# Value products of three key tiles in one visit to the TensorE queue, with a new table for the side work

## The chip, the cores and the metric

The kernel runs on one core of one Trainium2 chip. The metric is the device time of one execution in microseconds; lower is better. Before the change the median of 3 runs is 819.45 us (817.82 to 821.63).

## What is computed

Three blocks follow each other. The first, attention over 4 x 8 heads with the queries averaged in pairs, is where the change lies:

```python
q_pool = q.reshape(B, H, S // factor, factor, D).mean(axis=3)
scores = scale * np.matmul(q_pool, k.transpose(0, 1, 3, 2))
scores = scores - np.max(scores, axis=-1, keepdims=True)
attn = np.exp(scores)
attn = attn / (np.sum(attn, axis=-1, keepdims=True) + 1e-09)
return np.matmul(attn, v).astype(np.float32)
```

Sequence 1152 (576 pooled queries, 1152 keys), head width 64. The second block is a soft mixture of 8 experts over the 2304 resulting rows of 512 (logits `x @ phi`, softmax over the rows for the slots, softmax over the slots for the way back); the third is a gated feed-forward block with three weight matrices that arrive as 64-bit numbers.

## The kernel before

**Pairs and tiles.** Attention is done for 16 pairs of heads, p = 0 to 15. A pair has 9 key tiles of 128 keys (kt, 0 to 8), two heads (s) and two halves of 288 queries (h). For each (kt, s, h), `qk` issues two matmuls on TensorE (`sc`, L376 and L378): the product itself in split precision, with the negated row maximum as an extra row of the second. ScalarE takes the exponential (`e`, L384). GpSimd adds the `e` tiles of a head over the key tiles (`acc`, L413). `av` (L419) multiplies `e` by the values: for one tile and one half, two matmuls with 64 output rows each, one per head. A stretch of `av` matmuls between two stretches of scores is called a visit here.

**The maximum of the next pair.** While pair p is worked on, `max_tile` computes the plain scores of pair p+1 (`mxp`, L335) in 27 pieces, and VectorE reduces each (`mx`, L336). `max_row` turns the result (`mxw` on VectorE L340, `mxt` on TensorE L342, `mrow` on ScalarE L344) and `send_row` sends it with two small DMAs to where the second score matmul of the next pair reads it.

**Order.** Pairs 0 and 15 (`HALVED`) are done one query half at a time; pairs 1 to 14 follow the list `STEP`. In each key tile: four scores (`q0` to `q3`), a maximum piece after each (`m`; how many there are in which tile is in `MAX`), the value products of the tile before (`a0`, `a1`), the two additions (`e0`, `e1`). The products of the last tile follow right behind those of tile 7.

**Side work.** Everything else of the pairs around p is put between these steps by the table `AT`: a time of 4.59 means key tile 4, at the first step whose place in the list is past .59. Every engine works through its instructions in the order in which this program issues them. Among the side work: `low_k`, `low_q` (VectorE: the low parts of the split), `fill_w`, `spread_q`, `send_q`, `block_q`, `load_k/q/v` (DMAs, all from SyncE's queue), `sums` and `recips` (denominators), `x_turn`, `x_divide`, `x_logits`, `x_share`, `logit_add` (output rows and expert logits of pair p-1), the `d_` and `slot_` steps in p = 5, 9 and 13. The 64-bit weights are turned into 32-bit ones here, 36 tiles in all, called doubles below: `load_64` starts the DMA (up to three in a pair), `abs_64` does two ScalarE steps (L690, L692), and two `turn_64` steps on VectorE follow (L694, L695). Pairs 1 to 7, 9, 11 and 13 have three doubles, pairs 8, 10 and 12 two, pair 14 none.

**PSUM.** Scores, maximum pieces and all turned tiles share six banks (`bank`, tag `u`), given out in turn; `av` has two banks of its own. So TensorE can be at most six results ahead of the engines that read them.

Of the kernel before, what the change touches and what calls it, by code (L numbers as in the profile page):

```python
# [19 lines left out]
NKT = 9  # L20
# [7 lines left out]
NG = 6  # L28
NF = 12

STEP = "q0 m q1 m q2 m q3 m a0 a1 e0 e1".split()
MAX = [4, 4, 3, 4, 4, 4, 4, 0, 0]
EDV = []
XDV = []
AT = dict(
    spread_q=2.7,
    low_k=[0.6, 1.6],
    low_q=3.55,
    send_q=4.4,
    fill_w=[2.1, 3.2, 6.1],  # L40
    load_v=7.3,
    max_row=7.4,
    send_row=8.2,
    drop_k=7.0,
    load_q=4.3,
    load_k=5.73,
    sum_q=5.91,
    high_q=6.6,
    block_q=7.05,
    round_k=[7.8, 8.6],  # L50
    take_x=0.55,
    sums=2.6,
    recips=3.58,
    x_turn=[4.6, 5.6, 6.6],
    x_divide=[4.6, 5.6, 6.6],
    x_logits=7.6,
    x_share=8.3,
    logit_add=8.5,
    d_turn=0.59,
    d_exp=1.6,  # L60
    d_back=2.59,
    d_copy=3.55,
    slot_part=4.59,
    slot_copy=5.55,
    slot_turn=6.61,
    c_soft=[2.6, 4.6, 5.6],
    load_64=[0.86, 1.65, 4.0],
    abs_64=[2.6, 3.8, 7.6],
    turn_64=[3.6, 4.6, 5.6, 6.6, 7.1, 7.7, 8.1, 8.6],
    load_ew=[1.0, 3.4],  # L70
    load_14=[0.7, 1.7, 2.2, 2.7, 3.7, 4.2, 4.7, 5.7, 6.2, 7.7],
    load_15=[0.5, 1, 1.5, 2, 2.5, 3, 3.5, 4, 4.5, 5.5, 5.84, 6, 6.5, 7, 7.5, 8, 8.5],
)
AT_0 = dict(
    round_k1=[1.06, 1.56],
# [63 lines left out]
def attention_softmoe_gated_kernel(ctx: ExitStack, tc: tile.TileContext, kT, qT, vv, ip, cst, w1, w2, wg, wv, wo, rg, out):  # L139
# [640 lines left out]
    with tc.manual_schedule():  # L780
# [78 lines left out]
        for p in range(NP):  # L859
# [6 lines left out]
            for u, (kt, h) in enumerate(steps):  # L866
# [3 lines left out]
                for i, step in enumerate(order):  # L870
# [8 lines left out]
                    elif step == "m":  # L879
                        if mx < quota:  # L880
                            next_max(p, mx)
                            mx += 1
                    elif step[0] == "e":
                        add_e(p, kt, n, h)
                    elif h is None and kt:
                        av(p, kt - 1, n)
                    elif h is not None and u >= LAG:
                        av(p, *steps[u - LAG])
            for i, (kt, h) in enumerate(steps[-LAG:] if p in HALVED else ((NKT - 1, 0), (NKT - 1, 1))):
                if p == NP - 1 and i == LAG - 1:  # L890
                    sums(p, (1,))
                av(p, kt, h)
# [407 lines left out]
```

## Time and profile before

| | |
|---|---|
| median of 3 runs | 819.45 us |
| the profiled execution, its own time | 811.85 us |
| its span, first to last instruction | 810.1 us |
| busy in the span: TensorE matmul, VectorE, ScalarE, GpSimd | 763.3, 530.5, 474.2, 502.3 us |
| mean granted TensorE clock | 0.978 of full speed |
| pairs 1 to 14 | from 62.0 to 524.5 us |

The profile is of one execution. Its page gives for each engine the busy time and, per group of instructions, the number, the mean length and the idle time of the engine before them with what ended it. A row of the timeline gives the start, the length, the engine, the line, the operation, the tile written and read and, in brackets, the idle time before it. TensorE's matmuls overlap their successors, so the distance from start to start says more there than the length. An `av` matmul is recorded twice, since it is done in 32-bit floating point.

### The profile page before, as it was taken

The numbers are of one execution on the slowest core, as the hardware profiler recorded it, in microseconds if no ns is written. First come the engines' busy times: TensorE is split into PE (matmuls) and PEld (weight loads), VectorE is DVE, ScalarE is ACT, GpSimd is POOL, SyncE is SP. The second block draws the span as 40 slices with busy tenths as digits, with TensorE's granted clock in tenths as the row PEclk, the third lists the DMA queues.
The fourth block names the chain that finished last, engine by engine and source line by source line (L and its number), as shares of the span: only waits on it lengthen the run. The fifth ranks groups of instructions, "written<-read, shape, count | busy, mean of one in ns | idle before, by whom it ended". The sixth has DMA issues, their size and how long they took to land.

```text
span 810.1 us, 14487 instructions
## 1 busy us (share of the span) xinstructions
PE 763.3 (94%) x4861; PEld 536.4 (66%) x4861; DVE 530.5 (65%) x933; ACT 474.2 (59%) x1255; POOL 502.3 (62%) x393
## 2 busy tenths in 40 slices
PE   5889999999999999899998999998999999999998
PEld 4546667666566666566766667664436788888887
DVE  7648779887698887769778778555205575445330
ACT  3337777667667676666766666564316685645330
POOL 5557888786777888667877778742202785444330
PEclk8889999999999999999999999998999999999999
DMA  8668898898999999789898786657999010000001
GB/s 233 144 165 213 219 216 243 240 243 219 215 268 260 238 242 234 213 223 229 222 218 231 206 206 170 191 185 242 321 375 364 1 40 26 27 27 27 26 27 40
DMA packets 100875, 150.44 MB, mean 186 GB/s; under 512 B 28864, under 2 KB 61760, under 8 KB 100800
## 3 DMA queue, kind: packets, MB, share of 16 engines
q1 hardware_dynamic: 100800, 149.50, 66.3%
q8 instruction: 39, 0.64, 0.3%
q14 instruction: 36, 0.29, 0.1%
HBM read 89.39 MB, written 13.11 MB: 127 GB/s over the span
## 4 chain that ended last, share of the span: by engine, by line
PE 65%; DVE 14%; DMA 9%; issue 5%; ACT 3%; SPq 2%; POOL 1%; ACTq 0%; POOLq 0%; DVEq 0%
PE yo L1204 18%; PE av L419 12%; PE sc L376 9%; PE mxp L335 7%; DVE mx L336 6%; PE sc L378 6%; PE gv L1156 3%; DMA m<-mrow 3%; DVE w L694 2%; DVE qs L304 2%; DVE w L695 1%; PE xo L465 1%; DMA vt<-in_vv_dram 1%; PE hin L973 1%; ACT e L384 1%
## 5 line engine op out<-in xcount | busy, mean ns | idle before, releaser
L413 POOL TENSOR_TENSOR acc<-acc,e 128x576 f32<-128x576 f32 (+1 forms) x232 | 329.9, 1441 | 78.1 <-ACT e L384 77.1
L384 ACT ACTIVATE e<-sc 128x288 f32<-128x288 f32 x576 | 223.1, 413 | 163.7 <-PE sc L378 146.5
L336 DVE TENSOR_REDUCE mx<-mxp 128x1 f32<-128x384 f32 x432 | 216.2, 546 | 69.9 <-PE mxp L335 66.9
L376 PE MATMUL sc<-m,ws 128*128 128x288 f32 x576 | 192.6, 339 | 11.5 <-DVE mx L336 8.5
L378 PE MATMUL sc<-m,ws 65*128 65x288 f32 (+1 forms) x576 | 172.0, 303 | 6.7 <-DMA m<-mrow 6.1
L419 PE MATMUL av<-e,vt 128*64 128x288 f32 x1152 | 173.8, 423 | 0.0
L376 PEld LDWEIGHTS sc<-m,ws 128*128 128x128 f32 x576 | 111.5, 194 | 88.0 <-issue 36.3
L335 PE MATMUL mxp<-kh,bd 128*128 128x384 f32 x432 | 155.2, 368 | 12.8 <-DVE bd L809 6.8
L378 PEld LDWEIGHTS sc<-m,ws 65*128 65x128 f32 (+1 forms) x576 | 111.3, 193 | 8.4 <-DMA m<-mrow 4.7
L419 PEld LDWEIGHTS av<-e,vt 128*64 128x64 f32 x1152 | 70.1, 137 | 58.7 <-issue 27.3
L335 PEld LDWEIGHTS mxp<-kh,bd 128*128 128x128 f32 x432 | 85.0, 198 | 22.9 <-DVE mx L336 9.1
L1161 DVE SCALAR_TENSOR_TENSOR th<-th,gv 128x384 f32<-128x384 f32 x72 | 39.8, 553 | 61.9 <-ACT th L1158 61.3
L1204 PE MATMUL yo<-woh,hW 128*128 128x512 f32 (+1 forms) x228 | 73.9, 385 | 0.0
L1204 PE MATMUL yo<-woh,hA 128*128 128x512 f32 (+1 forms) x228 | 71.9, 380 | 0.0
L1187 POOL TENSOR_TENSOR hW<-hu,hW 128x384 fp32r<-128x384 f32 x36 | 36.5, 1016 | 49.8 <-ACT hW L1186 49.5
L413 POOL TENSOR_TENSOR acc<-e,e 128x576 f32<-128x576 f32 x28 | 40.7, 1473 | 39.8 <-ACT e L384 28.4
L1158 ACT ACTIVATE th<-gv 128x384 f32<-128x384 f32 x72 | 35.2, 488 | 42.8 <-PE gv L1156 40.2
L694 DVE SCALAR_TENSOR_TENSOR w<-w,raw 128x512 uint32<-128x512 uint32 x36 | 40.9, 1135 | 26.2 <-ACT raw L692 26.2
L1187 POOL TENSOR_TENSOR hA<-hu,hA 128x384 fp32r<-128x384 f32 x36 | 36.5, 1015 | 30.3 <-ACT hA L1186 25.9
L695 DVE SCALAR_TENSOR_TENSOR w<-raw,w 128x512 uint32<-128x512 uint32 x36 | 50.8, 1412 | 0.3
L474 ACT ACTIVATE xt<-xo,rr 96x64 f32<-96x64 f32 x186 | 42.5, 307 | 13.5 <-PE xo L465 12.4
L1204 PEld LDWEIGHTS yo<-woh,hW 128*128 128x128 f32 x228 | 42.1, 188 | 8.2 <-issue 0.7
(164 smaller groups left out, 943.4 us busy)
## 6 DMA issues: line engine op xcount, KB each, us to landing
w<-in_w_dram SPq DMA_DIRECT2D x88, 256.0 KB
ws<-kh SPq DMA_DIRECT2D x96, 192.0 KB
w<-in_w_dram SPq DMA_DIRECT2D x20, 512.0 KB
ws<-kraw SPq DMA_DIRECT2D x96, 96.0 KB
vt<-in_vv_dram SPq DMA_DIRECT2D x16, 576.0 KB
qraw<-in_qT_dram SPq DMA_DIRECT2D x15, 576.0 KB
m<-qh SPq DMA_DIRECT2D x60, 144.0 KB
kraw<-in_kT_dram SPq DMA_DIRECT2D x15, 576.0 KB
```

Of the source, the lines that this page charges most:

```text
L335: pe.matmul(o, lhsT=bds[p][:, t, :], rhs=kh[p][:, KC * c:KC * c + KC], start=True, stop=True)
L336: dv.reduce_max(out=mx3[p][:, t, c:c + 1], in_=o, axis=AX.X)
L376: pe.matmul(o, lhsT=w[:, s, 0, k], rhs=high_parts(p, s, h), start=True, stop=False)
L378: pe.matmul(o, lhsT=w[0:n, s, 1, k], rhs=low_parts(p, s, h)[0:n], start=False, stop=True)
L384: ac.activation(e, o, AF.Exp, scale=0.0625)
L413: eng.tensor_tensor(out=t, in0=a, in1=e, op=ALU.add)
L419: pe.matmul(avt[p, h][64 * s:64 * s + 64, 0:HQ], lhsT=vt[p][:, kt, 64 * s:64 * s + 64], rhs=ets[p, kt, s, h], start=(kt == 0), stop=(kt == ...
L474: ac.activation(xts[j // 3][:, j % 3, p % 4, c], o[:, i, c], AF.Copy, scale=r[:, j, s:s + 1])
L694: lambda y=y, lo=lo: dv.scalar_tensor_tensor(out=y, in0=y, scalar=3, in1=lo, op0=ALU.logical_shift_left, op1=ALU.bitwise_or),
L695: lambda y=y, hi=hi, key=key: (dv.scalar_tensor_tensor(out=y, in0=hi, scalar=0x80000000, in1=y, op0=ALU.bitwise_and, op1=ALU.bitwise_or), ...
L1187: gp.tensor_tensor(out=b, in0=u, in1=f(a), op=ALU.subtract)
L1204: pe.matmul(o, lhsT=x, rhs=w[:, c], start=(ft == 0 and i == 0), stop=(ft == NF - 1 and i == 2))
```

## The change

The two steps `a0 a1` of `STEP` become one step `a`, which does nothing except in tiles 2, 5 and 8: there it issues the value products of this tile and the two before it, both halves, tile by tile. The separate end for the last tile is gone. `av` itself is unchanged, and so is the number of its matmuls. `MAX` puts the tile with three maximum pieces at 6 instead of 2. Most times in `AT` are new. `AT_0` and `AT_15` take over the old values where pairs 0 and 15 need them, so that the side work of these two stands where it did. Two tiles of 128 x 576 more (`N_B`) and two of 128 x 512 fewer (`N_C`) are set aside. Lines of the changed kernel are 10 higher than before around `av` and the table's functions.

```diff
--- before.py
+++ after.py
@@ -28,48 +28,48 @@
 NG = 6
 NF = 12
 
-STEP = "q0 m q1 m q2 m q3 m a0 a1 e0 e1".split()
-MAX = [4, 4, 3, 4, 4, 4, 4, 0, 0]
+STEP = "q0 m q1 m q2 m q3 m a e0 e1".split()
+VISIT = 3
+MAX = [4, 4, 4, 4, 4, 4, 3, 0, 0]
 EDV = []
 XDV = []
 AT = dict(
     spread_q=2.7,
-    low_k=[0.6, 1.6],
-    low_q=3.55,
-    send_q=4.4,
-    fill_w=[2.1, 3.2, 6.1],
+    low_k=[2.7, 2.71],
+    low_q=5.65,
+    send_q=6.0,
+    fill_w=[4.0, 4.5, 6.1],
     load_v=7.3,
-    max_row=7.4,
-    send_row=8.2,
+    max_row=7.1,
+    send_row=7.9,
     drop_k=7.0,
     load_q=4.3,
     load_k=5.73,
-    sum_q=5.91,
-    high_q=6.6,
-    block_q=7.05,
-    round_k=[7.8, 8.6],
+    sum_q=6.05,
+    high_q=6.8,
+    block_q=7.35,
+    round_k=[7.8, 8.3],
     take_x=0.55,
-    sums=2.6,
+    sums=2.65,
     recips=3.58,
-    x_turn=[4.6, 5.6, 6.6],
-    x_divide=[4.6, 5.6, 6.6],
+    x_turn=[5.6, 5.61, 6.6],
+    x_divide=[5.7, 5.71, 6.7],
     x_logits=7.6,
-    x_share=8.3,
-    logit_add=8.5,
+    x_share=8.69,
+    logit_add=8.72,
     d_turn=0.59,
     d_exp=1.6,
     d_back=2.59,
     d_copy=3.55,
-    slot_part=4.59,
-    slot_copy=5.55,
-    slot_turn=6.61,
-    c_soft=[2.6, 4.6, 5.6],
-    load_64=[0.86, 1.65, 4.0],
-    abs_64=[2.6, 3.8, 7.6],
-    turn_64=[3.6, 4.6, 5.6, 6.6, 7.1, 7.7, 8.1, 8.6],
+    slot_part=5.55,
+    slot_copy=6.65,
+    slot_turn=7.65,
+    c_soft=[2.72, 4.6, 5.68],
+    load_64=[0.86, 1.65, 6.5],
+    abs_64=[2.73, 6.3, 7.9],
+    turn_64=[5.69, 6.7, 7.2, 7.7, 8.2, 8.65, 8.7],
     load_ew=[1.0, 3.4],
     load_14=[0.7, 1.7, 2.2, 2.7, 3.7, 4.2, 4.7, 5.7, 6.2, 7.7],
-    load_15=[0.5, 1, 1.5, 2, 2.5, 3, 3.5, 4, 4.5, 5.5, 5.84, 6, 6.5, 7, 7.5, 8, 8.5],
 )
 AT_0 = dict(
     round_k1=[1.06, 1.56],
@@ -81,6 +81,15 @@
     high_q=6.19,
     round_k=[7.91, 8.72],
     max_row=7.63,
+    load_v=7.3,
+    drop_k=7.0,
+    load_q=4.3,
+    load_k=5.73,
+    sum_q=5.91,
+    block_q=7.05,
+    send_row=8.2,
+    abs_64=[2.6, 3.8, 7.6],
+    turn_64=[3.6, 4.6, 5.6, 6.6, 7.1, 7.7, 8.1, 8.6],
 )
 AT_15 = dict(
     take_x=0.24,
@@ -102,6 +111,7 @@
     d_back_a=7.62,
     slot_part_a=8.2,
     slot_turn_a=9.43,
+    load_15=[0.5, 1, 1.5, 2, 2.5, 3, 3.5, 4, 4.5, 5.5, 5.84, 6, 6.5, 7, 7.5, 8, 8.5],
 )
 MAX_0 = [2, 4, 2, 1, 2, 4, 3, 3, 3, 3, 3, 1, 4, 2, 2, 0, 0, 0]
 HALVED = (0, 15)
@@ -117,8 +127,8 @@
 TAIL = [(0, 2), (2, 2)]
 N_W = 6
 N_A = 8
-N_B = 18
-N_C = 40
+N_B = 20
+N_C = 38
 KEEP_B = 4
 EARLY = 4
 LEAD = 1
@@ -882,11 +892,14 @@
                             mx += 1
                     elif step[0] == "e":
                         add_e(p, kt, n, h)
-                    elif h is None and kt:
-                        av(p, kt - 1, n)
+                    elif h is None:
+                        if kt % VISIT == VISIT - 1:
+                            for k in range(kt - VISIT + 1, kt + 1):
+                                av(p, k, 0)
+                                av(p, k, 1)
                     elif h is not None and u >= LAG:
                         av(p, *steps[u - LAG])
-            for i, (kt, h) in enumerate(steps[-LAG:] if p in HALVED else ((NKT - 1, 0), (NKT - 1, 1))):
+            for i, (kt, h) in enumerate(steps[-LAG:] if p in HALVED else ()):
                 if p == NP - 1 and i == LAG - 1:
                     sums(p, (1,))
                 av(p, kt, h)
```

The next blocks show the order of instructions on three engines. First TensorE, pair 8, at the end of tile 7. Before (the last row of the logits `xl` of pair 7, then the visit that does the products of tile 6; `e0` and `e1` are the two heads, the two `av` tiles the two halves):

```order
L481 MATMUL xl_4043<-ipt_72,xu_3701 96x64 x6
L419 MATMUL av_3747<-e1_3988,vt_3598 64x288
L419 MATMUL av_3747<-e0_3969,vt_3598 64x288
L419 MATMUL av_3750<-e1_3988,vt_3598 64x288
L419 MATMUL av_3750<-e0_3969,vt_3598 64x288
L376 MATMUL sc_4062<-m10_3371,ws_102 128x288
```

The changed kernel has scores alone around these logits, and its next visit is that after tile 8:

```order
L429 MATMUL av_3796<-e1_3993,vt_3600 64x288
L429 MATMUL av_3796<-e0_3969,vt_3600 64x288
L429 MATMUL av_3799<-e1_3993,vt_3600 64x288
L429 MATMUL av_3799<-e0_3969,vt_3600 64x288
L429 MATMUL av_3796<-e1_4036,vt_3600 64x288
L429 MATMUL av_3796<-e0_4017,vt_3600 64x288
L429 MATMUL av_3799<-e1_4036,vt_3600 64x288
L429 MATMUL av_3799<-e0_4017,vt_3600 64x288
L429 MATMUL av_3796<-e1_4073,vt_3600 64x288
L429 MATMUL av_3796<-e0_4063,vt_3600 64x288
L429 MATMUL av_3799<-e1_4073,vt_3600 64x288
L429 MATMUL av_3799<-e0_4063,vt_3600 64x288
```

Four matmuls of one tile became twelve of three; the last four read exponentials of the scores that stand just ahead of the visit.

Second ScalarE, pair 7, from the second half of tile 6 on. Before:

```order
L384 ACTIVATE e_3559<-sc 128x288 x2
L268 CAST qh<-qs 128x576
L474 ACTIVATE xt<-xo,rr 96x64 x4
L384 ACTIVATE e_3590<-sc 128x288 x2
L384 ACTIVATE e_3603<-sc 128x288
L344 ACTIVATE mrow<-mxt 9x128
L384 ACTIVATE e_3603<-sc 128x288
L690 ACTIVATE w_3625<-raw_3439 128x512
L692 ACTIVATE raw_3439<-raw_3439 128x512
L259 CAST kh<-kraw 128x576
L384 ACTIVATE e_3640<-sc 128x288 x2
L384 ACTIVATE e_3654<-sc 128x288 x2
```

And changed (the first row belongs to another double, whose two steps now stand in tile 6):

```order
L702 ACTIVATE raw_3312<-raw_3312 128x512
L394 ACTIVATE e_3562<-sc 128x288 x2
L484 ACTIVATE xt<-xo,rr 96x64 x4
L278 CAST qh<-qs 128x576
L394 ACTIVATE e_3588<-sc 128x288
L354 ACTIVATE mrow<-mxt 9x128
L394 ACTIVATE e_3588<-sc 128x288
L394 ACTIVATE e_3607<-sc 128x288 x2
L269 CAST kh<-kraw 128x576
L700 ACTIVATE w_3630<-raw_3567 128x512
L702 ACTIVATE raw_3567<-raw_3567 128x512
L394 ACTIVATE e_3637<-sc 128x288 x2
```

Two doubles instead of one stand between the exponentials of tiles 6 to 8, and the load of the later one (`raw_3567`) is issued in tile 6, where that of `raw_3439` was issued in tile 4.

Third VectorE, pair 7, from tile 5 on. Before:

```order
L336 TENSOR_REDUCE mx_3247<-mxp 128x1 x4
L695 SCALAR_TENSOR_TENSOR w_3366<-raw_3277,w_3366 128x512
L336 TENSOR_REDUCE mx_3247<-mxp 128x1 x4
L694 SCALAR_TENSOR_TENSOR w_3434<-w_3434,raw_3314 128x512
L336 TENSOR_REDUCE mx_3247<-mxp 128x1 x4
L695 SCALAR_TENSOR_TENSOR w_3434<-raw_3314,w_3434 128x512
L340 TENSOR_REDUCE mxw<-mx_3247 128x9
L694 SCALAR_TENSOR_TENSOR w_3625<-w_3625,raw_3439 128x512
L695 SCALAR_TENSOR_TENSOR w_3625<-raw_3439,w_3625 128x512
L492 TENSOR_TENSOR ls<-xl,rr 96x384
L502 TENSOR_TENSOR lg<-lg,ls 96x192
L503 TENSOR_TENSOR lg<-lg,ls 96x192
```

And changed:

```order
L314 TENSOR_TENSOR qs<-qs,qh 128x576
L704 SCALAR_TENSOR_TENSOR w_3381<-w_3381,raw_3276 128x512
L346 TENSOR_REDUCE mx_3247<-mxp 128x1 x3
L705 SCALAR_TENSOR_TENSOR w_3381<-raw_3276,w_3381 128x512
L350 TENSOR_REDUCE mxw<-mx_3247 128x9
L704 SCALAR_TENSOR_TENSOR w_3556<-w_3556,raw_3312 128x512
L705 SCALAR_TENSOR_TENSOR w_3556<-raw_3312,w_3556 128x512
L704 SCALAR_TENSOR_TENSOR w_3630<-w_3630,raw_3567 128x512
L705 SCALAR_TENSOR_TENSOR w_3630<-raw_3567,w_3630 128x512
L502 TENSOR_TENSOR ls<-xl,rr 96x384
L512 TENSOR_TENSOR lg<-lg,ls 96x192
L513 TENSOR_TENSOR lg<-lg,ls 96x192
```

Five of the six steps that finish doubles now stand behind the last maxima, one of them between these and the row maximum `mxw`; `low_q` (L304, now L314) moved from tile 3 to tile 5.

## Rows read from the trace of the kernel before

**Rows 1.** Stretches: length; busy PE, PEld, DVE, ACT, POOL (instructions); clock; DMA share, GB/s.

```profile
62.00:188.40 126.40, 122.06 (x806) 85.41 (x804) 105.03 (x164) 90.38 (x244) 103.77 (x69) 1.00 0.87 229
226.20:291.10 64.90, 62.32 (x405) 42.60 (x403) 55.52 (x90) 45.71 (x123) 52.15 (x34) 1.00 0.94 251
291.10:323.40 32.30, 30.67 (x203) 21.28 (x201) 27.34 (x42) 21.42 (x59) 26.29 (x19) 1.00 0.94 243
361.60:394.00 32.40, 31.18 (x204) 21.31 (x202) 27.38 (x47) 22.00 (x60) 26.29 (x18) 1.00 0.93 241
426.20:460.30 34.10, 31.30 (x204) 22.70 (x202) 26.50 (x43) 21.61 (x59) 28.50 (x20) 0.95 0.80 212
494.90:524.50 29.60, 29.57 (x204) 21.31 (x202) 22.59 (x43) 17.75 (x53) 23.60 (x17) 1.00 0.67 178
```

**Rows 2.** Waits between 62 and 524.5 us: waiter and releaser, us, times, longest.

```profile
PEld sc L376 <- DVE mx L336: 19.9, 37, 1.2
...
PE sc L378 <- DMA m<-mrow: 6.1, 7, 2.1
```

**Rows 3.** Timeline of TensorE, pair 7, the visit in tile 1.

```profile
263.01 0.34 PE L335 MATMUL mxp<-kh,bd 128*128 128x384 f32 x1
263.28 1.19 PE L419 MATMUL av<-e,vt 128*64 128x288 f32 x8
264.40 0.40 PE L376 MATMUL sc<-m,ws 128*128 128x288 f32 x1
264.63 0.30 PE L378 MATMUL sc<-m,ws 65*128 65x288 f32 x1
264.77 0.34 PE L335 MATMUL mxp<-kh,bd 128*128 128x384 f32 x1
264.95 0.29 PE L376 MATMUL sc<-m,ws 128*128 128x288 f32 x1
265.08 0.30 PE L378 MATMUL sc<-m,ws 65*128 65x288 f32 x1
```

**Rows 4.** Timeline of TensorE, pair 7, tile 6: a turn before a visit.

```profile
282.61 0.38 PE L465 MATMUL xo<-cs,xu 128*96 128x128 f32 x2
282.92 1.19 PE L419 MATMUL av<-e,vt 128*64 128x288 f32 x8
```

**Rows 5.** Timeline of TensorE, pair 7, tiles 7 and 8.

```profile
284.82 0.30 PE L378 MATMUL sc<-m,ws 65*128 65x288 f32 x1
285.09 0.33 PE L342 MATMUL mxt<-cs,mxw 128*128 128x128 f32 x1
285.17 0.38 PE L376 MATMUL sc<-m,ws 128*128 128x288 f32 x1
285.39 0.29 PE L378 MATMUL sc<-m,ws 65*128 65x288 f32 x1
285.52 1.15 PE L481 MATMUL xl<-ipt,xu 128*96 128x64 f32 x12
...
289.01 2.16 PE L419 MATMUL av<-e,vt 128*64 128x288 f32 x16
```

**Rows 6.** Timeline of ScalarE, pair 7, tiles 6 to 8.

```profile
283.50 0.91 ACT L474 ACTIVATE xt<-xo,rr 96x64 f32<-96x64 f32 x4
...
286.03 0.67 ACT L690 ACTIVATE w<-raw 128x512 f32<-128x512 f32 x1
...
288.30 1.32 ACT L384 ACTIVATE e<-sc 128x288 f32<-128x288 f32 x4 [0.47 <-PE sc L378]
```

**Rows 7.** Timeline of VectorE, pair 7, tile 6, to the start of pair 8.

```profile
283.28 1.65 DVE L695 SCALAR_TENSOR_TENSOR w<-raw,w 128x512 uint32<-128x512 uint32 x1
...
287.30 0.83 DVE L694 SCALAR_TENSOR_TENSOR w<-w,raw 128x512 uint32<-128x512 uint32 x1 [2.27 <-ACT raw L692]
...
292.93 1.95 DVE L336 TENSOR_REDUCE mx<-mxp 128x1 f32<-128x384 f32 x4
```

**Rows 8.** Chain that ended last, 180 to 196 us: start, us, what.

```profile
187.88 6.87 DMA raw<-in_wv_dram
```

## Prediction

> **What bounds the kernel now.** I read the table of stretches first, one stretch per pair or run of pairs. In [rows 1] the reader sees TensorE busy for 30.7 to 31.3 of 32 to 34 us in an ordinary pair, VectorE for 26 to 28, ScalarE for 22, GpSimd for 26: TensorE sets the pace, VectorE is close behind. The clock column says 1.00, the 2.4 GHz level, in all but one of these stretches (0.95 in pair 12), so the clock is no part of the change. Pair 14 issues the same 204 matmul records as its neighbours and has no doubles: it takes 29.6 us, all of it busy. Pairs 1 to 4, 6 and 7, each with three doubles, take 191.3 / 6 = 31.9; pairs 8, 10 and 12, with two, 98.8 / 3 = 32.9. What is over 29.6 is waiting: 2.3 and 3.3 us per pair. The waits say on whom: VectorE's maxima above all, whose banks the next scores need, and sometimes the small DMA with the row maxima [rows 2].
>
> **What a visit costs.** In [rows 3] the scores follow `av` 1.12 us after its start; the visit with two tiles [rows 5] lasts 2.16 against 1.19, so one tile's products are 0.97 and 0.15 is fixed. The step into the visit takes 0.27 (263.01 to 263.28) where the same piece is otherwise followed by scores after 0.18 (264.77 to 264.95): 0.09. The first score pair behind it has 0.23 between its halves (264.40 to 264.63), otherwise 0.13 (264.95 to 265.08): 0.10. A visit costs 0.15 + 0.09 + 0.10 = 0.34 us beside its products.
>
> **What the change removes of it.** A pair has 8 visits, and then 3. Those in tiles 1, 3 and 4 vanish whole: 3 x 0.34 = 1.02. Those in tiles 6 and 7 leave the turn `xo` and the logits `xl` behind, which shared their entry: in [rows 4] two turns and the step into the visit take 0.31 together. An isolated 32-bit turn is `mxt` in [rows 5]: from the second half before it to the second half behind it 0.57 (284.82 to 285.39), where two steps of 0.13 to 0.14 make 0.27; with 0.11 for the turn itself (half of what [rows 4] leave after the 0.09) 0.19 is fixed. So these two give 2 x (0.34 - 0.19) = 0.30. The turns of tiles 4 and 5, both attached to a visit, become one group with a maximum piece between it and the visit: -0.19. Sum 1.02 + 0.30 - 0.19 = 1.13 us per pair, **15.8 us** in 14 pairs. The ends: if isolated turns cost nothing, 5 x 0.34 = 1.70 less per pair, 23.8 us; if they cost as much as a visit, 1.02 - 0.34 = 0.68, 9.5 us. I take the middle one because `mxt` is the nearest row.
>
> The Trainium skill, TensorEngine Tiling, section Key Properties, says that a change of the array's tiling drains TensorE, while another tile of the same tiling does not. By that rule the turns, which are not split into 64-column tiles, would be free between scores, and the gain would be 23.8 us; the `mxt` row, 0.19 us for one, speaks against it and decides here.
>
> **What it moves: the first six tiles.** Without visits between them four scores and four maximum pieces take 4 x 0.45 = 1.8 us per tile (0.27 for a score pair, 0.18 for the piece), while VectorE needs 1.95 for its four maxima when nothing holds it up (those that begin at 292.93 [rows 7]). The 0.15 more per tile is 0.45 in three tiles, the length of one score pair and piece, and the six banks hold three. That fits as long as nothing else stands between the maxima, and in the new order of tiles 0 to 5 only the two reciprocal steps and, in tile 5, `low_q` and one step of a double do; `low_k` stands in front of the first visit, `low_q` near the second, each with three tiles' products, 3 x 0.97 + 0.34 = 3.2 us, as cover. If that cover were gone they would hold up the maxima as `low_q` in tile 3 does now. I cost these moves at nothing. `fill_w` of the next pair goes from tiles 2 and 3 to tile 4, still five tiles before its use; `send_row` goes 0.3 tiles ahead and has a longer visit behind it, so the 6.1 us of [rows 2] may shrink; `load_q` and `load_k` stay.
>
> **The last three tiles are the dear part.** Count from the first score of tile 6. TensorE reaches `mxt` after four score pairs, three pieces, 0.10 for the first pair, two turns (0.41) and one more pair: 5 x 0.27 + 3 x 0.18 + 0.10 + 0.41 = 2.4 us. The third piece starts at 1.27, is 0.34 long, and its maximum takes 1.95 / 4 = 0.49: VectorE is through at 2.1. Then a double's step of 1.65 [rows 7] stands before `mxw`: `mxt` starts at 3.8, a wait of 1.4 that before lay behind the visit of tile 6. The rest (seven pairs 1.9, `mxt` 0.3, `xl` 1.15 [rows 5] and 0.2) brings the last visit to 7.3. ScalarE up to the end of its second double has 8 exponentials at 1.32 / 4 = 0.33, the divisions 0.91, two casts and four halves of doubles at 0.67 [rows 6]: 2.6 + 0.9 + 4.0 + 0.4 for the start = 7.9; four exponentials and a cast make it 9.9. The products that need them come 1.94 after the start of the visit, at 9.2. So ScalarE is late by some tenths and the group ends at about 10.6 with 1.6 us of waiting. VectorE, from the end of a double on ScalarE to the first maximum of the next pair, takes 292.93 - 287.30 = 5.6 us [rows 7]: 7.9 + 5.6 = 13.5, 2.9 behind the end of the group. Before it is 1.8 behind (the visit ends at 289.01 + 2.16 = 291.17). TensorE can be three pieces ahead, reaches the fourth at 1.7 us, and needs the first maximum done, at 2.9 + 0.49 = 3.4: a wait of 1.7.
>
> **The sum.** Pairs with three doubles: waits 1.6 + 1.7 = 3.3 instead of 2.3, against 1.13 gained: -0.13, times 10 (5, 9 and 13 taken like the others) -1.3. Pairs with two: no second double in tile 8, VectorE is through before the pair ends; waits 1.6 instead of 3.3: -1.7 - 1.13 = -2.8, times 3 -8.5. Pair 14: -1.1. Together -10.9: 811.85 - 10.9 = 800.95 for the profiled execution. Its own time lies 7.6 below the median of the runs, so the median becomes 819.45 - 10.9 = **808.5**. What comes after pair 15 moves unchanged; two fewer small buffers and two more large ones I count as nothing.
>
> **The rivals.**
> *A: the waits of the last group do not come.* For it: VectorE's step before `mxw` was as short as 0.83 in [rows 7] for its sister, and ScalarE's list was counted at full lengths. Then 1.4 us less in 13 pairs, 18 us: 790.5. Against: the order puts that step there in every pair with a double.
> *B: slower, by the load of the third double.* It is now issued in tile 6, behind the four DMAs of `fill_w`, and ScalarE wants it at 7.9 - 1.34 = 6.6 us, in front of tile 8's exponentials. A load of this kind took 6.87 us [rows 8]. Issued at the start of the group it costs 0.3; every microsecond later costs one in ten pairs, and beyond 1.1 us the gain is gone. At 2.5: -10.9 + 25 = +14.1, 833.5. For it: a DMA share of 0.94 at 251 GB/s [rows 1]. Against: SyncE has nothing to wait for there but its own issues.
> *C: nothing.* VectorE's 26 to 28 us of work in a pair of 28.5 leave it hardly any idle time, and the pairs with two doubles keep their DMA waits: only about 3 us go, 816.5. For it: all lumps stand at one place now.
>
> The Trainium skill, same page, section PSUM Bottleneck, warns that a faster TensorE leaves the emptying of PSUM as the bound; C is that rule at work on this kernel, and [rows 1] are consistent with it without showing it.
>
> **How the numbers follow.** The forecast (802 to 814) gets 0.53, A (786 to 798) 0.20, C (813 to 819) 0.14, B (826 and more) 0.13. What is under 0.5% can't be told from no change: 815.4 to 823.5 is "same". Faster: the forecast, less a little for its upper end, and A: 0.70. Same: C and that little: 0.16. Slower: B and its neighbours: 0.14. The range 789 to 823 takes in the forecast, C and over half of A; the forecast's own range is 802 to 814.
>
> **What would show it.** Three visits of 3.1 us per pair, with scores again 3 x 0.97 + 0.15 = 3.06 behind their start; an isolated `xo` or `xl` with about 0.2 us fixed; pair 14 at 28.5. A wait of TensorE on `mxw` of about 1.4 us in tile 7, and on the first maxima at the start of a pair after three doubles. Tiles 0 to 5 without waits on VectorE. I would be wrong if pair 14 stays at 29.6 (then a visit has no fixed price), if ScalarE stands idle in front of L700 until a DMA lands (B), or if waits on maxima fill tiles 0 to 5 (C).

## The result and the profile after

| | before | after |
|---|---|---|
| median (18 runs each, taken together) | 817.49 us | 825.12 us |
| ratio after / before | | 1.0108, 95% interval 1.0078 to 1.0138 |
| profiled execution, span | 811.85, 810.1 us | 822.46, 820.7 us |
| mean granted clock of the profiled execution | 0.978 | 0.947 |
| TensorE, VectorE, ScalarE, GpSimd busy | 763.3, 530.5, 474.2, 502.3 us | 760.4, 565.6, 469.2, 507.7 us |
| pairs 1 to 14, first score to first score | 462.5 us | 473.3 us |
| of it: TensorE idle in gaps over 0.05 us | 19.9 us | 33.3 us |
| of it: clock at the 1.2 GHz level | 3.4 us | 59.0 us |

The change makes the kernel 1.1% slower; 808.5 us had been forecast. All of it arises in pairs 1 to 14. The clock differs in every run: 0.930 to 0.952 in the 18 of the change, 0.966 to 0.989 in the 80 on record of the kernel before.

The stretches of the change that answer to [rows 1] (length; busy PE, PEld, DVE, ACT, POOL; clock; DMA share, GB/s): pairs 1 to 4, 6 and 7, 8, 12, and 14.

```profile
60.90:197.30 136.40, 124.69 (x806) 93.80 (x804) 119.99 (x166) 89.47 (x244) 106.18 (x68) 0.91 0.82 213
233.10:301.90 68.80, 62.09 (x405) 46.65 (x403) 60.34 (x91) 44.74 (x123) 54.12 (x35) 0.92 0.88 243
301.90:336.20 34.30, 32.53 (x203) 24.64 (x201) 30.48 (x42) 21.18 (x59) 27.14 (x18) 0.87 0.90 243
438.60:470.00 31.40, 28.64 (x204) 21.62 (x202) 29.43 (x42) 21.18 (x59) 26.25 (x17) 1.00 0.80 205
504.40:534.10 29.70, 28.31 (x203) 21.82 (x201) 26.52 (x45) 17.73 (x53) 24.89 (x18) 1.00 0.66 173
```

Two columns have changed. VectorE works 30 us per pair instead of 26 to 28, on the same steps. And the clock, 1.00 in nearly every stretch before, is at 0.87 to 0.92 in three of these five. In the other two, pairs 12 and 14, TensorE is busy for 28.6 and 28.3 us, where it was 31.3 and 29.6 before: the visits are saved. Only pair 14 compares like with like, since 3.4 us of pair 12 passed at the lower clock before.

Waits of the change between 60.9 and 534.1 us (waiter and releaser: us, times, longest), to be held against [rows 2]:

```profile
PE mxt L352 <- DVE mxw L350: 14.8, 13, 1.5
PEld av L429 <- ACT e L394: 12.3, 9, 4.5
PEld sc L386 <- DVE mx L346: 11.5, 22, 2.2
...
PE av L429 <- ACT e L394: 8.5, 5, 4.0
ACT kh L269 <- issue: 7.4, 4, 1.9
...
ACT kh L269 <- DVE w L705: 3.1, 2, 1.6
```

The scores wait less for maxima than in [rows 2], and the 6.1 us on the row of maxima are gone. In their place TensorE waits 14.8 us for `mxw` in tile 7 and, in a few pairs, for the exponentials of the last visit. The wait of ScalarE's cast `kh` is behind the second of these.

Where the time is lost shows when a pair is cut into three groups of tiles (0 to 2, 3 to 5, 6 to 8; sums over pairs 1 to 14, us, worked out from the starts of the scores; before, the visit at a cut lies one tile later):

| | tiles 0-2 | tiles 3-5 | tiles 6-8 | 1.2 GHz in tiles 6-8 |
|---|---|---|---|---|
| before | 138.2 | 174.2 | 150.1 | 0 |
| after | 145.9 | 140.8 | 186.6 | 54.6 |

The timeline of TensorE in pair 2, tiles 6 to 8 of the change (start, us, what):

```profile
117.67 0.30 PE L388 MATMUL sc<-m,ws 65*128 65x288 f32 x1
119.43 0.30 PE L352 MATMUL mxt<-cs,mxw 128*128 128x128 f32 x1 [1.45 <-DVE mxw L350]
...
120.75 2.07 PE L491 MATMUL xl<-ipt,xu 128*96 128x64 f32 x12
...
124.78 4.06 PE L429 MATMUL av<-e,vt 128*64 128x288 f32 x24
128.78 0.40 PE L386 MATMUL sc<-m,ws 128*128 128x288 f32 x1
```

VectorE in the same stretch:

```profile
117.31 1.89 DVE L705 SCALAR_TENSOR_TENSOR w<-raw,w 128x512 uint32<-128x512 uint32 x1
119.12 0.17 DVE L350 TENSOR_REDUCE mxw<-mx 128x9 f32<-128x27 f32 x1
```

And the stretches ahead of and behind 119.9 us (columns as above):

```profile
115.00:119.90 4.90, 3.41 (x21) 2.54 (x20) 4.90 (x7) 4.30 (x13) 4.90 (x4) 1.00 0.84 181
119.90:126.70 6.80, 6.80 (x33) 5.61 (x33) 4.81 (x4) 4.92 (x12) 5.34 (x4) 0.50 0.91 256
```

VectorE's step L705 holds up `mxw`, TensorE stands for 1.45 us, and from 119.9 us on the granted clock is 0.50, the 1.2 GHz level, for 6.8 us in which TensorE is busy without a gap. `xl` takes 2.07 us there against 1.15 in [rows 5], the last visit 4.06 with most of it at the low level. Nine such stretches, of 3.4 to 10.2 us, lie in pairs 1 to 14. In pairs 1, 2, 3, 8 and 11 they begin 0.5 to 1.4 us after the end of the gap before `mxt`, in pairs 6 and 10 after waits of 1.7 and 1.9 us on a piece of maxima in tile 6, in pairs 4 and 7 near waits of 4.0 and 3.0 us on exponentials. Pairs 4, 7 and 12 have the gap of 1.45 us too and the clock does not fall right behind it, so the gap makes the fall likely and not certain.

The kernel before had one such stretch, in pair 12. TensorE waited 2.11 us for the row maxima there, and the clock was low from 1.6 us after the wait:

```profile
428.71 0.40 PE L378 MATMUL sc<-m,ws 65*128 65x288 f32 x1 [2.11 <-DMA m<-mrow]
```

```profile
430.30:433.70 3.40, 3.40 (x15) 3.24 (x13) 3.16 (x7) 2.29 (x8) 1.12 (x1) 0.50 0.48 105
```

This is what lies behind the 0.95 of [rows 1]: a fall of the clock behind a wait was already in the trace of the kernel before.

The second wait, in pair 4: ScalarE, the waits in brackets.

```profile
189.42 0.67 ACT L269 CAST kh<-kraw 128x576 fp32r<-128x576 f32 x1 [1.86 <-issue]
192.49 0.66 ACT L700 ACTIVATE w<-raw 128x512 f32<-128x512 f32 x1 [2.40 <-DMA raw<-in_wv_dram]
```

VectorE's step before it, and SyncE's own waits on that line (L652 is the load of a double):

```profile
187.55 1.79 DVE L705 SCALAR_TENSOR_TENSOR w<-raw,w 128x512 uint32<-128x512 uint32 x1
```

```profile
SPq L652 <- DVE w L705: 7.4, 7, 1.5
```

The cast starts as L705 ends (187.55 + 1.79 = 189.34): it writes a buffer that this step frees. Behind the cast, in ScalarE's order, stand the third double and tile 8's exponentials. The third double's load needs such a buffer as well, so SyncE waits on the same line, and in pair 4 ScalarE then waits 2.40 us more for the data.

Why VectorE is late: its largest groups in pairs 1 to 14 (line, shape and count; busy us, mean ns; idle before). First before, then after.

```profile
L336 DVE TENSOR_REDUCE mx<-mxp 128x1 f32<-128x384 f32 x378 | 189.1, 545 | 54.9 <-PE mxp L335 52.0
L695 DVE SCALAR_TENSOR_TENSOR w<-raw,w 128x512 uint32<-128x512 uint32 x36 | 50.8, 1412 | 0.3
L694 DVE SCALAR_TENSOR_TENSOR w<-w,raw 128x512 uint32<-128x512 uint32 x36 | 40.9, 1135 | 26.2 <-ACT raw L692 26.2
L317 DVE TENSOR_TENSOR kraw<-kraw,kh 128x576 fp32r<-128x576 f32 x28 | 34.4, 1229 | 0.0
```

```profile
L346 DVE TENSOR_REDUCE mx<-mxp 128x1 f32<-128x384 f32 x378 | 182.0, 543 | 36.2 <-PE mxp L345 35.6
L705 DVE SCALAR_TENSOR_TENSOR w<-raw,w 128x512 uint32<-128x512 uint32 x36 | 59.2, 1644 | 0.7
L704 DVE SCALAR_TENSOR_TENSOR w<-w,raw 128x512 uint32<-128x512 uint32 x36 | 52.2, 1450 | 21.8 <-ACT raw L702 21.8
L327 DVE TENSOR_TENSOR kraw<-kraw,kh 128x576 fp32r<-128x576 f32 x28 | 47.1, 1721 | 0.0
```

The maxima last as long as before. The steps with two inputs in SBUF grew by 16 to 40%: on the three lines together 158.5 us instead of 126.1, 32.4 more. `low_k` (L317, now L327) took 0.74 to 0.75 us in 14 of its 28 steps before and in 3 of 28 after: the step is the same, its place is not. What GpSimd has to do with it is tested below.

### The profile page after: what moved, and what is told of

The parts are those of the page before. It is cut to its first block, busy times and chain, and to the rows that moved or that the text cites. A ratio compares the mean times of both kernels' runs of the same rounds, so it can differ in the third digit from the quotient of the medians.

```text
span 820.7 us, 14457 instructions
## 1 busy us (share of the span) xinstructions
PE 760.4 (93%) x4861; PEld 558.5 (68%) x4861; DVE 565.6 (69%) x933; ACT 469.2 (57%) x1255; POOL 507.7 (62%) x393
## 4 chain that ended last, share of the span: by engine, by line
PE 63%; DVE 16%; DMA 10%; ACT 4%; issue 4%; POOL 2%; SPq 1%; ACTq 0%; DVEq 0%; POOLq 0%
PE yo L1217 18%; PE av L429 11%; PE sc L386 8%; PE sc L388 6%; PE mxp L345 6%; DVE mx L346 5%; DVE qs L314 3%; PE gv L1169 3%; DVE w L704 2%; ACT e L394 2%; DMA w<-in_w_dram 2%; DMA ws<-kraw 2%; PE xl L491 2%; PE hin L986 1%; PE so L1009 1%
## 5 line engine op out<-in xcount | busy, mean ns | idle before, releaser
L423 POOL TENSOR_TENSOR acc<-acc,e 128x576 f32<-128x576 f32 (+1 forms) x232 | 333.7, 1463 | 78.0 <-ACT e L394 76.9
L394 ACT ACTIVATE e<-sc 128x288 f32<-128x288 f32 x576 | 224.0, 412 | 167.7 <-PE sc L388 154.4
L346 DVE TENSOR_REDUCE mx<-mxp 128x1 f32<-128x384 f32 x432 | 209.1, 544 | 47.0 <-PE mxp L345 46.0
L388 PE MATMUL sc<-m,ws 65*128 65x288 f32 (+1 forms) x576 | 178.3, 312 | 1.6 <-DMA m<-mrow 1.5
L429 PE MATMUL av<-e,vt 128*64 128x288 f32 x1152 | 171.5, 441 | 8.5 <-ACT e L394 8.5
L386 PEld LDWEIGHTS sc<-m,ws 128*128 128x128 f32 x576 | 117.2, 203 | 57.8 <-issue 26.1
L429 PEld LDWEIGHTS av<-e,vt 128*64 128x64 f32 x1152 | 80.4, 146 | 78.8 <-issue 29.3
L388 PEld LDWEIGHTS sc<-m,ws 65*128 65x128 f32 (+1 forms) x576 | 116.8, 203 | 2.3 <-issue 1.7
L1200 POOL TENSOR_TENSOR hW<-hu,hW 128x384 fp32r<-128x384 f32 x36 | 36.6, 1018 | 50.8 <-ACT hW L1199 44.4
L704 DVE SCALAR_TENSOR_TENSOR w<-w,raw 128x512 uint32<-128x512 uint32 x36 | 52.2, 1450 | 21.8 <-ACT raw L702 21.8
L705 DVE SCALAR_TENSOR_TENSOR w<-raw,w 128x512 uint32<-128x512 uint32 x36 | 59.2, 1644 | 0.7
L327 DVE TENSOR_TENSOR kraw<-kraw,kh 128x576 fp32r<-128x576 f32 x30 | 49.0, 1669 | 0.3 <-ACT kh L269 0.3
```

The costliest lines, as they stand in the source:

```text
L327: eng.tensor_tensor(out=kraw[p].bitcast(F32R)[:, c], in0=kraw[p][:, c], in1=f(kh[p][:, c]), op=ALU.subtract)
L346: dv.reduce_max(out=mx3[p][:, t, c:c + 1], in_=o, axis=AX.X)
L386: pe.matmul(o, lhsT=w[:, s, 0, k], rhs=high_parts(p, s, h), start=True, stop=False)
L388: pe.matmul(o, lhsT=w[0:n, s, 1, k], rhs=low_parts(p, s, h)[0:n], start=False, stop=True)
L394: ac.activation(e, o, AF.Exp, scale=0.0625)
L423: eng.tensor_tensor(out=t, in0=a, in1=e, op=ALU.add)
```

## The experiments

**Theory.** The visits do save at least what was forecast. But the new table puts the doubles, both casts and the row maxima into tiles 6 to 8; VectorE's steps are long there, TensorE waits for them, and these waits let the clock fall, which costs about as much again. **Rivals:** the new table, not the visits, is the loss (or the reverse); the clock follows from the waits and costs nothing of its own; VectorE is simply full.

### Each half of the change alone

The visits with the old table, the old `MAX` and a list of old length:

```diff
+                        if kt % VISIT == VISIT - 1 and n == 0:
+                            for k in range(kt - VISIT + 1, kt + 1):
+                                av(p, k, 0)
+                                av(p, k, 1)
...
```

The separate end for the last tile falls away as in the change, and the small buffers (`N_B`, `N_C`) are those of the change; these lines are not shown.

> One part alone: the visits of three tiles with the table, the maximum pieces and the step list of the kernel before. Both theories: 1.13 us per pair of visit cost go (15.8 us). The list theory: tiles 6 to 8 have the shorter lists of before, so the third groups come out at 9 to 10.5 us without low clock, but low_k, low_q and the doubles now stand between maxima without a visit behind each tile and cost 1 to 2 us in each of the first two groups: ratio 0.985 to 1.00. The clock theory: the waits are spread, none is long enough for the clock: the same ratio, with under 15 us at the low level.

The table and `MAX` of the change with a visit per tile:

```diff
-                        if kt % VISIT == VISIT - 1:
-                            for k in range(kt - VISIT + 1, kt + 1):
-                                av(p, k, 0)
-                                av(p, k, 1)
+                        if kt:
+                            av(p, kt - 1, 0)
+                            av(p, kt - 1, 1)
...
```

The separate end for the last tile is back, as before the change (not shown).

> The other part alone: the table, the maximum pieces and the reserves of the changed kernel, with one visit per tile as before. The list theory: the lists of tiles 6 to 8 are as long as in the changed kernel but TensorE has a visit more in each of tiles 6 and 7, so the wait on the row maximum is covered by the visit of tile 6 and the third group takes 11.5 to 12.5 us: ratio 1.00 to 1.01. The clock theory: without the wait in tile 7 there is no low level in pairs 1 to 14 (under 10 us) and the ratio is 0.99 to 1.00.

Measured: visits alone 854.31 us, ratio 1.0467 (1.0396 to 1.0538); table alone 839.69, 1.0252 (1.0169 to 1.0334). Both lie far above what either theory forecast for them. Waits with the table alone:

```profile
PEld sc L386 <- DVE mx L346: 43.1, 43, 4.1
...
PE sc L386 <- DVE mx L346: 26.5, 16, 3.8
```

Each half alone is worse than both together, so neither is "the" loss. With the old table the time goes in tiles 3 to 5 (212.7 us, 64.9 of them at 1.2 GHz), while tiles 6 to 8 take 132.8, 9.4 in an ordinary pair. With the new table and old visits the scores wait for maxima: what covered `low_k` and `low_q`, a visit of three tiles, is missing.

### The row maxima ahead of the double

```diff
-    turn_64=[5.69, 6.7, 7.2, 7.7, 8.2, 8.65, 8.7],
+    turn_64=[5.69, 7.12, 7.2, 7.7, 8.2, 8.65, 8.7],
```

> The changed kernel with one time moved: the second step of the first double goes from 6.7 to 7.12, so VectorE does the row maximum first and this step behind it. The clock theory (the wait of 1.45 us on the row maximum, 14.8 us in 13 pairs, lets TensorE's granted clock fall to the 1.2 GHz level for some 59 us of pairs 1 to 14, and that is what made the change slower): the wait goes to under 3 us in all, the time at the low level to under 15 us, and the kernel comes out at 0.975 to 0.985 of the kernel before. The list theory (ScalarE and VectorE have more to do in tiles 6 to 8 than TensorE has there, and the clock only follows): the wait goes, another on exponentials takes its place, the third groups stay over 13 us, the low level stays over 35 us, and the ratio is 1.00 to 1.01.

Measured: 826.99 us, 1.0109 (1.0064 to 1.0154), no gain, close to what the list theory forecast. Its waits:

```profile
PE av L429 <- ACT e L394: 21.5, 9, 4.3
...
ACT kh L269 <- issue: 16.2, 7, 2.5
```

The wait for `mxw` is gone and has moved: L705 now ends later, the cast waits 16.2 us for its buffer, and the last visit 21.5 us for exponentials. The clock is low for 44.4 us.

### The gap filled with useless products

Eleven copies of the first score product of tile 7, written to the bank that the real product then overwrites:

```diff
+        for _ in range(FILL if 0 < p < NP - 1 and (kt, s, h) == (7, 0, 0) else 0):
+            pe.matmul(o, lhsT=w[:, s, 0, k], rhs=high_parts(p, s, h), start=True, stop=True)
```

> The changed kernel with eleven extra copies of a score matmul in front of the first score of tile 7 in pairs 1 to 14 (each writes the bank that the real one then overwrites; 288 columns, 0.12 us). They fill the 1.45 us in which TensorE waits for the row maximum with work that waits for nothing. The clock theory: the place in time of all other work stays, but the granted clock no longer falls there; under 15 us at the low level in pairs 1 to 14, ratio to the kernel before 0.985 to 0.995. The list theory: no gain, ratio 1.01 to 1.02.

Measured: 814.38 us, 0.9971 (0.9925 to 1.0016), 1.4% less than the change and a little above the forecast range. TensorE in pair 2 (line numbers are 1 to 3 higher in this kernel):

```profile
119.76 1.71 PE L388 MATMUL sc<-m,ws 128*128 128x288 f32 x11
...
121.76 0.30 PE L353 MATMUL mxt<-cs,mxw 128*128 128x128 f32 x1
...
122.71 1.16 PE L494 MATMUL xl<-ipt,xu 128*96 128x64 f32 x12
```

The copies take 1.71 us where the wait took 1.45, and `xl` takes 1.16 instead of 2.07. The time at 1.2 GHz in pairs 1 to 14 falls from 59.0 to 13.7 us, that of tiles 6 to 8 from 186.6 to 175.8. More work for TensorE made the kernel faster: the clock has a price of its own, and the rival falls. How large it is: from start to start the 154 copies take 23.6 us in pairs 1 to 14, the gaps shrink by 7.4, and the pairs are 6.8 us shorter all the same. So 45.3 us less at the low level were worth about 6.8 + 23.6 - 7.4 = 23.0 us, an estimate of half a microsecond for each.

### The casts behind the exponentials, without and with the copies

```diff
-    round_k=[7.8, 8.3],
+    round_k=[8.71, 8.712],
```

> The changed kernel with the two casts round_k moved from 7.8 and 8.3 to just behind tile 8's exponentials. In the changed kernel the first of them writes a buffer that the second vector step of a double frees, waits for it on ScalarE, and tile 8's exponentials stand behind it. The buffer theory: ScalarE no longer waits there, the wait of the last visit on the exponentials (20.8 us of TensorE in pairs 1 to 14 with its weight loads) goes to under 6 us; the wait of 1.45 us on the row maximum stays and with it some of the low clock: ratio to the kernel before 0.995 to 1.005. The full-VectorE theory (its work of 30 us and more per pair sets the pace, whatever waits for it): what is gained there comes back as waits on maxima in the next pair's first tiles, ratio 1.005 to 1.015.

> Both edits: the casts behind tile 8's exponentials and the row maximum ahead of the double's second step. The buffer and clock theories together: neither wait is left in tiles 6 to 8, the third groups come down from 13.3 us on average to 10 to 11, under 20 us of pairs 1 to 14 are at the low level, ratio 0.965 to 0.985. The full-VectorE theory: the pairs with three doubles stay at 31 us or more because VectorE needs that, waits stand at the first maxima of a pair (over 1 us each), the clock falls there instead, ratio 0.99 to 1.01.

Measured: casts late 825.86 us, 1.0155 (1.0113 to 1.0197); with the row maxima first as well 822.93, 1.0055 (1.0008 to 1.0103). With the casts late the products hardly wait for exponentials any more, but one wait of 1.45 us before `mxt` stays in most pairs, pieces of maxima wait 0.6 to 1.8 us in tiles 0 and 6, and 47.8 us are at 1.2 GHz. Order alone does not mend it: the first ratio is a little above what the theory of a full VectorE forecast, the second in its range. Then the copies, at one place and at two:

```diff
+        for _ in range(FILL if 0 < p < NP - 1 and (kt, s, h) == (7, 0, 0) or (p, kt, s, h) in ((6, 6, 1, 1), (10, 6, 1, 1)) else 0):
```

> The change with both rounding casts behind tile 8's exponentials, and with 11 useless copies of the first score product of tile 7, which keep TensorE busy while the turn of the row maxima waits 1.45 us for VectorE. Theory (the wait itself is cheap, the drop of the clock behind it is dear, and the exponentials are late only because a cast stands ahead of them): the third group of a pair takes 11.5 us instead of 12.4 (the casts late, no copies: 174.2 us in 14 pairs, 44.4 us of it at the 1.2 GHz level) , the time at that level in pairs 1 to 14 falls below 25 us, and the kernel is 10 to 20 us faster than with the casts late alone: 806 to 815, a ratio of 0.985 to 0.997. Rival (VectorE and ScalarE are full, the clock follows from their waits and costs nothing of its own): the same time as with the casts late alone, 823 to 828, ratio 1.005 to 1.012.

> The one before with 11 more copies ahead of the last score of tile 6 in pairs 6 and 10, where a piece of row maxima waits 1.8 us for VectorE and the clock falls for 6.8 and 10.2 us behind it. Theory: these two stretches stay at 2.4 GHz, 3 to 8 us less than with the copies at one place. Rival: no difference beyond 2 us, since VectorE, which is waited for there, is no sooner done.

Measured: 813.69 us, 0.9954 (0.9924 to 0.9984), the only kernel with all the work done whose interval lies below the kernel before, and faster than the change; and 816.03, 0.9959 (0.9916 to 1.0003). The eleven copies are all that differs from the kernel with late casts, and they give 2.0% in the ratio.

The second place gained nothing in the medians, and its edit does not test its theory. The copies write the very bank that TensorE waits for, so in pair 10 they stand behind the wait and not in it, and the one low stretch that is left is there (the copies, then the stretch):

```profile
379.64 2.87 PE L388 MATMUL sc<-m,ws 128*128 128x288 f32 x11 [1.81 <-DVE mx L347]
```

```profile
379.80:383.20 3.40, 3.40 (x16) 3.35 (x16) 2.70 (x6) 0.17 (x1) 0.59 (x1) 0.50 1.07 203
```

With the copies at one place the profile has 3.4 us at the low level in pair 10, none in pair 6, and 10.2 us in the first tiles of pairs 3 and 4. That these 10.2 are gone here (pairs 1 to 14 in 460.6 us) can't be the second place's work, which touches pairs 6 and 10 alone; the profiled execution is also the fastest of its kernel's twelve.

### VectorE's and GpSimd's part, each left out

The change, and the kernel before, without the 72 vector steps of the doubles (so the converted weights are not finished):

```diff
-                lambda y=y, lo=lo: dv.scalar_tensor_tensor(out=y, in0=y, scalar=3, in1=lo, op0=ALU.logical_shift_left, op1=ALU.bitwise_or),
-                lambda y=y, hi=hi, key=key: (dv.scalar_tensor_tensor(
-                    out=y, in0=hi, scalar=0x80000000, in1=y, op0=ALU.bitwise_and, op1=ALU.bitwise_or), rel("A"),
-                    done.append(key) if key in out_of_chip else None),
+                lambda: None,
+                lambda key=key: (rel("A"), done.append(key) if key in out_of_chip else None),
```

> The changed kernel without the 72 vector steps of the doubles (L704, L705: the weights of the last block keep the wrong bits, all else is as it was; some 110 us of VectorE work are gone). The visit theory, that a visit's fixed 0.34 us is really saved: pairs without extra steps take 28.0 to 29.0 us, no low clock in pairs 1 to 14, and against the kernel before without these steps the time is 0.975 to 0.985. If visits save nothing: 29.5 us or more per pair and no difference between the two. Ratio to the kernel before 0.93 to 0.96.

> The kernel before without the same 72 vector steps, as the other's partner. The visit theory: its pairs take 29.6 us as pair 14 does, with few waits; ratio to the kernel before 0.955 to 0.975. If VectorE is not what holds the pairs up even before: 30.5 us or more per pair, ratio over 0.98.

> The change without the 72 vector steps of the doubles, once more, for a profile at the usual clock (the profile of the first was taken at 0.65). If the waits of the last group come from these steps, its third groups take 10 to 11 us with no wait on VectorE, and the time at the 1.2 GHz level in pairs 1 to 14 is under 20 us; if ScalarE's list alone is too long for the group, products still wait on exponentials there.

Measured: the change without them 805.95 us, 0.9844 (0.9801 to 0.9888), and again 801.75, 0.9799 (0.9718 to 0.988); the kernel before without them 817.99, 0.996 (0.9906 to 1.0015). The first two lie above the forecast 0.93 to 0.96, and the last above 0.98: VectorE isn't what holds up the kernel before. Pair 14 of the change, which has no doubles (the profile of the second run; below it the matmul in it that waits):

```profile
480.80:509.30 28.50, 27.84 (x204) 21.59 (x202) 24.74 (x42) 17.30 (x53) 23.38 (x17) 1.00 0.70 186
```

```profile
503.04 0.30 PE L352 MATMUL mxt<-cs,mxw 128*128 128x128 f32 x1 [0.54 <-DVE mxw L350]
```

and of the kernel before:

```profile
497.50:527.10 29.60, 29.58 (x203) 21.30 (x201) 22.44 (x42) 17.77 (x53) 23.02 (x17) 1.00 0.65 179
```

With VectorE relieved the change gains 2.6 to 3.1% against its own ratio of 1.0108, the kernel before 0.4%. Between the two stand 1.2 to 1.6% in the ratios, 9 to 13 us, and 465.5 - 443.5 = 22 us in pairs 1 to 14 of the profiles. That is nearer to the prediction's upper end for the visits, 23.8, than to the 15.8 that it took; the gaps of the two differ by 2.2 us and their time at 1.2 GHz by 3.5. Pair 14 says the same: it is 1.1 us shorter than before although TensorE waits 0.54 us in it for `mxw`, and without that wait it would take about 27.96, 1.6 less than before. 12.2 us of waits on exponentials remain; in part they are ScalarE's list and in part late loads, for which ScalarE waited 9.0 us in this run.

Last, the change without the 196 GpSimd additions of tiles 2 to 8 in pairs 1 to 14 (the denominators lack these tiles):

```diff
-        eng.tensor_tensor(out=t, in0=a, in1=e, op=ALU.add)
+        if p in HALVED or kt == 1:
+            eng.tensor_tensor(out=t, in0=a, in1=e, op=ALU.add)
```

> The change without the 196 GpSimd additions of the exponentials of key tiles 2 to 8 in pairs 1 to 14 (the row sums lack them); VectorE keeps every step. Theory (VectorE is late in tiles 6 to 8 because its steps of two inputs take 1.7 to 1.9 us beside a GpSimd addition, against 0.69 alone): the two steps of a double take under 0.9 us in the mean (1.45 and 1.64 with the additions), the turn of the row maxima waits under 0.4 us instead of 1.45, the time at 1.2 GHz in pairs 1 to 14 falls from 59 to under 25 us, and the kernel is at 790 to 805, a ratio of 0.965 to 0.985. Rival (the steps are slow by themselves, or by the DMA traffic): steps as long as now, waits as now, 820 to 828.

Measured: 793.42 us, 0.9698 (0.9627 to 0.9769). VectorE's groups (line numbers are 1 higher from L424 on):

```profile
L346 DVE TENSOR_REDUCE mx<-mxp 128x1 f32<-128x384 f32 x382 | 184.6, 545 | 101.1 <-PE mxp L345 100.8
L706 DVE SCALAR_TENSOR_TENSOR w<-raw,w 128x512 uint32<-128x512 uint32 x36 | 25.2, 700 | 0.7
L705 DVE SCALAR_TENSOR_TENSOR w<-w,raw 128x512 uint32<-128x512 uint32 x36 | 24.7, 686 | 37.6 <-ACT raw L703 37.6
L327 DVE TENSOR_TENSOR kraw<-kraw,kh 128x576 fp32r<-128x576 f32 x28 | 19.8, 746 | 0.0
```

VectorE keeps every step, and those with two inputs take 0.69 to 0.75 us instead of 1.45 to 1.72, the maxima 0.545 as ever. `mxt` waits 0.25 us in most pairs and 0.74 at most, 10.7 us are at 1.2 GHz, and tiles 6 to 8 take 154.4 us instead of 186.6. So VectorE was late because of the GpSimd instructions beside its steps. DMA traffic is no rival: its share is higher here than in the change, 0.90 against 0.81 in pairs 1 to 14, and the steps are short. Eight waits on exponentials, 17.3 us, are left, the longest 6.74 in pair 4, behind the late load of the third double. Pair 14, where TensorE waits 0.24 us for `mxw`:

```profile
479.68:507.52 27.84, 27.56 (x204) 21.65 (x202) 18.30 (x42) 17.12 (x53) 2.80 (x2) 1.00 0.74 194
```

| pairs 1 to 14, us | length | gaps of TensorE | at 1.2 GHz |
|---|---|---|---|
| before | 462.5 | 19.9 | 3.4 |
| after | 473.3 | 33.3 | 59.0 |
| copies | 466.5 | 25.9 | 13.7 |
| casts late | 471.0 | 31.4 | 47.8 |
| casts late, copies | 464.3 | 24.3 | 13.7 |
| before, no vector steps of doubles | 465.5 | 22.5 | 13.7 |
| after, no vector steps of doubles | 443.5 | 24.7 | 10.2 |
| after, no additions | 442.1 | 26.1 | 10.7 |

The two rows without vector steps or additions of the change have gaps too, mostly late exponentials, and little time at the low level.

## Why the prediction was wrong

**The cost of a visit: right; what is left of it without the visit: sized too large.** Scores follow the start of a visit in tile 2 of pair 2 after 105.06 - 102.00 = 3.06 us, as forecast. TensorE's rows there:

```profile
102.00 3.13 PE L429 MATMUL av<-e,vt 128*64 128x288 f32 x24
105.06 0.40 PE L386 MATMUL sc<-m,ws 128*128 128x288 f32 x1
```

Pair 14 was forecast at 28.5, and the 28.50 above is a hit by luck: 0.54 of it is the wait for `mxw`. Without the wait the pair takes 27.96, and 27.84 in the run without additions, a wait of 0.24 included. That is the prediction's other end, "if isolated turns cost nothing", 27.9 for the pair and 23.8 us in 14 pairs. The 0.19 fixed for an isolated turn was read from the `mxt` of [rows 5], and that one had waited for VectorE: `mxw` ended at 284.86 + 0.17 = 285.03, `mxt` started at 285.09.

```profile
284.86 0.17 DVE L340 TENSOR_REDUCE mxw<-mx 128x9 f32<-128x27 f32 x1
```

In pair 14 of the same kernel the same stretch takes 518.77 - 518.39 = 0.38, which is the 0.27 of two steps and the 0.11 of the turn, with nothing fixed:

```profile
518.39 0.30 PE L378 MATMUL sc<-m,ws 65*128 65x288 f32 x1
518.53 0.27 PE L342 MATMUL mxt<-cs,mxw 128*128 128x128 f32 x1
...
518.77 0.30 PE L378 MATMUL sc<-m,ws 65*128 65x288 f32 x1
```

The Trainium skill, TensorEngine Tiling, section Key Properties, by which only a change of the tiling drains TensorE, would have made the pair 29.6 - 1.70 = 27.9; the 27.96 and 27.84 above agree. In the change itself pair 14 takes 29.7, which the prediction named as a sign that a visit has no fixed price; but TensorE is busy for 28.31 of it, and the rest are waits, the longest 0.61 and 0.54 us.

**Tiles 0 to 5 at no cost: right.** Tiles 3 to 5 take 9.6 us in an ordinary pair, without a wait on VectorE. The 1.7 us forecast for the first maxima of a pair after three doubles mostly did not come (0.75 us in pair 10, 0.61 in pair 14), likely because TensorE is so late that VectorE has caught up by then; no run separates this.

**The wait for `mxw`: right in size.** 1.4 forecast, 1.45 measured in eight pairs and 0.25 to 1.1 in the others that have it, 14.8 us in all.

**"The clock is no part of the change": this step failed first.** Its price was put at nothing. It was read from the column of [rows 1], held for the kernel before only, and passed over the 0.95 of pair 12, which lay behind a wait. The forecast made one place where TensorE stands still in tile 7 and asked what the wait cost, not what it does to the clock. The runs showed 59.0 us at 1.2 GHz in pairs 1 to 14 instead of 3.4, most of it behind waits in tiles 6 to 8. Balance for these pairs: +10.8 us measured, -23.8 for the visits (the prediction's end with free turns), +13.4 for more gaps (33.3 - 19.9); what is left, 21.2 us, is an estimate of the clock's price. The copies' half a microsecond for each one at the low level makes it 28 for the 55.6 us more. So the clock cost some 21 to 28 us, about as much as the visits gained.

**ScalarE and SyncE in the last group: sized too small.** "ScalarE is late by some tenths" counted its own steps and no wait. It waits for L705, whose buffer its cast needs, and SyncE, which had "nothing to wait for there but its own issues", waits 7.4 us on the same line. So rival B came in part, late loads of 2.40 us in pair 4 and 1.42 in pair 7. By the prediction's own figures ScalarE could be 0.7 us late (9.9 against 9.2), of which its 1.6 us of waiting counted 0.2 beyond the wait for `mxw`. Forecast for all waits were +4.9 us net (15.8 - 10.9); they are +13.4.

**VectorE's durations: taken from where they stood, not from where they go.** A double's step of 1.65 us was a fair figure; that `low_k` and the others would lengthen by up to 40% was not considered. It brought VectorE to 30 us per pair and made rival C's condition true, a full VectorE, though the time then came out on the other side of C because of the clock.

What stays open: why the clock falls behind the gap of 1.45 us in pairs 1, 2, 3, 8 and 11 and not in 4, 7 and 12. No run was made for it. Nor did a run part ScalarE's own list from the late loads in the waits on exponentials.

## What to carry to other kernels

Saving time on the engine that sets the pace is worth little if the rest is then packed into one place: give each engine its list there, with buffers and their releasers, before counting the gain. Ask of every new wait of TensorE not only how long it is but whether the clock holds behind it; where the wait can't be removed, a few useless products in it can be cheaper, provided they don't wait for the same thing. Before a row is taken as the price of an instruction, look what the engine waited for there. And read the length of a vector step together with what GpSimd does beside it, since moving the step changes it.

## What the hardware showed

**Two-input steps beside GpSimd.** A step of VectorE with two SBUF inputs of 512 elements took 0.69 us alone and 1.45 to 1.64 in the mean among GpSimd's additions, up to 1.9; a reduction that reads a PSUM bank took 0.545 us either way. GpSimd's additions took 1557 ns before and 1582 after, and 1468 and 1483 where the doubles' vector steps were left out: about 0.1 us for each of 196, an estimate of 20 us, against some 61 us that the doubles' 72 steps took more than alone (59.2 + 52.2 - 25.2 - 24.7). So VectorE bears most of the cost, and GpSimd a part. The Trainium skill, SBUF — State Buffer, section SBUF: two separate sides, says that a VectorE instruction with two SBUF inputs and a GpSimd instruction that reads SBUF exclude each other for a whole instruction, and that others of VectorE's are not touched. The runs agree on both counts.

**The clock after short waits.** Gaps of 1.45 us, with TensorE busy on both sides, were followed by 6.8 us at 1.2 GHz in five of eight pairs; with eleven useless products in the gap 13.7 us at that level were left in pairs 1 to 14 instead of 59.0. The kernel before had one, 3.4 us behind a wait of 2.11.

**Visits and turns.** A visit of 64-column value products between scores cost 0.34 us beside its products. A single 32-bit turn between scores that waited for nothing cost its 0.11 us and nothing fixed (0.38 us from score to score in pair 14 of the kernel before, where two steps without it take 0.27).
